# One weight load of a decode kernel, issued as two DMAs of 100 and 28 partitions

## The chip, the core and the metric

The kernel runs on one core of a Trainium2 chip. The metric is the device time of one execution in microseconds (us). The core has TensorE (PE in the profile), VectorE (DVE), ScalarE (ACT), GpSimd (POOL) and SyncE (SP), each with its own list of instructions; they meet at semaphores. Here SP issues nearly all DMAs, and sixteen DMA engines carry the bytes between HBM and the on-chip memory of 128 partitions.

## The reference

One decode step of a transformer block, for four sequences of one token each, width 512, in bfloat16:

```
x    = A_x                                                  # (4, 1, 512)
q    = layernorm(x) @ wq                                    # 32 heads of 128
p    = softmax(q . k_cache * 128**-0.5)                     # caches (4, 32, 8192, 128)
h    = x + (p . v_cache) @ wo
hn   = layernorm(h)
out  = h + (sigmoid(hn @ w_gate) * (hn @ w_up)) @ w_down    # 512 -> 1792 -> 512
```

The two caches are 512 MiB together; all weights are some 13 MB.

## The kernel before

**Attention.** The 128 pairs of sequence and head are taken four at a time, so there are 32 units (`NU`). A unit's K and its V are 8 MiB each and come in one DMA each into one of three slots of the tensor `KV`. For each unit DVE transposes K in chunks (L320), PE forms the scores (L329), DVE and ACT form the softmax (L336 to L356), and PE multiplies with V of the unit before (L368, L381). The loads are written in one fixed order in SP's list (`order`, L224): K of unit 0, then K of the next unit and V of the one before in turn. Each waits until its slot is free. The last V comes in two halves (L492).

**The tail.** When the last K has been read (`k_done`, L335 of the last unit), SP issues the weights into that slot: `wo` in two DMAs (L501), `w_gate` in one (L503) and `w_up` in two (L507). Then, when the slot of V is free (`v_done`), `w_down` follows in four (L512). All go through one queue, in this order, without a wait between them but `v_done`. `w_up` lies as 128 partitions of 4 x 1792 elements; the cut `WUC = (0, 3, 4)` gives the first load three of the four chunks `c` (10752 B a partition) and the second load one (3584 B a partition). `w_down` is cut at `WDT = (0, 4, 8, 12, 14)` of its fourteen tiles `t`.

The tail's arithmetic: PE finishes attention and multiplies with `wo` (L431), DVE and ACT form the layernorm (L266 to L270), PE transposes the result (L276), then multiplies with `w_gate` and `w_up` (both L446, four chunks `c` each). ACT takes the sigmoid (L457), which needs a table load first. DVE multiplies (L463) and transposes (L466), in two halves of seven tiles. PE multiplies with `w_down` (L471, two matmuls for each of fourteen tiles), the tiles in order, each group waiting for its load. DVE adds `h` (L477), and two small DMAs write the output (L514).

**Semaphores.** `prog.token(key, 16)` (L27) raises the count that a key is expected to reach by 16 and gives the value to wait for; `prog.dma` (L82) issues a DMA that adds 16 to the semaphore of that key when it is complete. The token of the second up load is `t_wu[1]`; PE's second group of up matmuls (L460) waits for it.

## Time and profile before

| | |
|---|---|
| median of 3 runs | 1281.62 us (1281.55 to 1281.74) |
| the profiled execution's own time | 1281.89 us |
| its span, first to last instruction | 1280.1 us |
| DMA | 550.83 MB, mean 430 GB/s |
| PE busy, matmuls | 789.8 us (62%) |
| DVE busy | 797.5 us (62%) |
| ACT busy | 55.2 us (4%) |
| mean granted TensorE clock | 0.811 of full speed |
| second up load: size, median issue to landing | 448 KB, 21.1 us |

The times in profile and trace are counted in us from the first instruction of the span. The page gives busy time by engine, then the span in 40 equal slices with a digit each (9 is 90% or more busy), then the DMA queues with packets, MB and their share of the time of sixteen DMA engines. The chain of work that ended last is followed back from the last instruction, at each step to what released it. In a timeline a row is start, length, engine, line, operation, tile and count, and in brackets how long the engine sat idle before it and what ended that. SPq is SP issuing DMAs: the length of such a row is the issue, not the transfer. Beside these views the trace holds every packet of the DMA engines (start, length, bytes, queue, but no engine number), and every increment of a semaphore by a DMA, here called a landing event.

### The profile page before, as it was taken

The page shows a single profiled execution, that of the slowest core. Times are in us where ns is not written, and L with a number is a line of the kernel's source. Part 1 is how long each engine was busy: PE and PEld are TensorE (multiplying, and loading weights), DVE is VectorE, ACT ScalarE, POOL GpSimd, SP SyncE. Part 2 cuts the span into 40 slices and gives each one's busy share as a digit, 9 for nine tenths or more (in the row PEclk, how much of TensorE's full clock was granted, in tenths as well). Part 3 has the DMA queues.
Part 4 walks back from the last instruction along what each step waited for, and adds up shares of the span by engine and source line. Part 5 has one row for each costly group of instructions (what it writes and reads, how often), then busy time and mean ns, then how long its engine had stood idle before and what let it go on. Part 6 is the DMA issues. An engine that isn't in the chain of part 4 may idle for free. (4 is left out here: it accounts for less than half of the span.)

```text
span 1280.1 us, 10700 instructions
## 1 busy us (share of the span) xinstructions
PE 789.8 (62%) x4485; PEld 292.0 (23%) x4485; DVE 797.5 (62%) x1075; ACT 55.2 (4%) x112; POOL 4.3 (0%) x18
## 2 busy tenths in 40 slices
PE   1676755557755557655557655567655577555586
PEld 0122212222212222212222212222122222122232
DVE  1876675567675567665567665566765666755671
ACT  2000000000000000000000000000000000000001
POOL 1000000000000000000000000000000000000000
PEclk8888877788877788877788877788777888777887
DMA  9999999999999999999999999999999999999998
GB/s 420 431 425 428 451 430 428 426 442 440 426 428 432 451 426 428 428 451 430 428 426 440 442 426 428 432 451 426 428 428 448 432 428 426 440 442 426 428 426 341
DMA packets 11596, 550.83 MB, mean 430 GB/s; under 512 B 1212, under 2 KB 1224, under 8 KB 2888
## 3 DMA queue, kind: packets, MB, share of 16 engines
q1 hardware_dynamic: 11576, 550.77, 99.6%
q8 instruction: 3, 0.05, 0.0%
q10 hardware_dynamic: 16, 0.01, 0.0%
q14 instruction: 1, 0.01, 0.0%
HBM read 550.77 MB, written 0.00 MB: 430 GB/s over the span
## 5 line engine op out<-in xcount | busy, mean ns | idle before, releaser
L329 PE MATMUL PS<-kT,Lq 128*128 128x512 bf16 x2048 | 587.9, 419 | 439.0 <-DVE kT L320 420.6
L320 DVE STREAM_TRANSPOSE kT<-KV 128x1024 f32<-128x1024 f32 x512 | 612.1, 1230 | 239.5 <-DMA KV<-in_A_k_cache_dram 192.1
L329 PEld LDWEIGHTS PS<-kT,Lq 128*128 128x128 bf16 x2048 | 176.9, 104 | 848.3 <-DVE kT L320 684.4
L368 PE MATMUL PS<-KV,PTz 128*16 128x512 bf16 x2048 | 120.5, 389 | 6.7 <-DVE PTz L349 3.5
L386 DVE STREAM_TRANSPOSE kT<-PS 128x128 f32<-128x128 f32 x32 | 10.1, 317 | 161.3 <-PE PS L381 161.3
L349 DVE STREAM_TRANSPOSE PTz<-E_sb 32x512 bf16<-32x512 bf16 x128 | 89.7, 701 | 3.6 <-ACT E_sb L343 0.6
L381 PE MATMUL PS<-kT,selw 128*128 128x128 f32 x256 | 66.3, 415 | 24.9 <-ACT kT L377 24.9
L368 PEld LDWEIGHTS PS<-KV,PTz 128*16 128x16 bf16 x2048 | 59.4, 110 | 65.6 <-issue 16.4
L343 ACT ACTIVATE E_sb<-PS,negm 128x512 bf16<-128x512 f32 x32 | 22.0, 687 | 1144.5 <-DVE negm L341 1144.5
L381 PEld LDWEIGHTS PS<-kT,selw 128*128 128x128 f32 x256 | 49.8, 206 | 43.9 <-ACT kT L377 40.8
L336 DVE TENSOR_REDUCE part<-PS 128x1 f32<-128x512 f32 x32 | 22.1, 692 | 35.8 <-PE PS L329 35.8
L377 ACT ACTIVATE kT<-PS 128x512 f32<-128x512 f32 x32 | 19.1, 598 | 61.1 <-PE PS L368 61.1
L387 DVE TENSOR_SCALAR OT<-kT,rsb 128x4 f32 (+1 forms) x32 | 7.3, 229 | 4.4
L313 DVE TENSOR_TENSOR Lq<-q_all,mask 128x32 bf16<-128x32 bf16 x32 | 9.6, 301 | 0.0
L431 PE MATMUL PS<-KV,OT 128*4 128x512 bf16 x32 | 8.4, 429 | 0.0
L341 DVE STREAM_TRANSPOSE negm<-mxr 128x32 f32<-128x32 f32 x32 | 6.8, 213 | 1.1
L338 DVE STREAM_TRANSPOSE turn<-part 128x32 f32<-128x32 f32 x32 | 6.8, 211 | 1.1
L356 DVE STREAM_TRANSPOSE rsb<-sgr 128x32 f32<-128x32 f32 x32 | 6.8, 211 | 1.1
L353 DVE STREAM_TRANSPOSE turn<-part 128x32 f32<-128x32 f32 x32 | 6.8, 212 | 1.0
L294 PE MATMUL PS<-KV,kT 128*4 128x512 bf16 x32 | 3.6, 627 | 5.4 <-DMA KV<-in_A_wq_dram 5.4
L339 DVE TENSOR_SCALAR_CACHE_REDUCE turn<-turn 128x32 f32<-128x32 f32 x32 | 5.9, 186 | 1.1
L301 DVE STREAM_TRANSPOSE kT<-PS 128x512 f32<-128x512 f32 x2 | 1.4, 717 | 8.2 <-PE PS L294 8.2
(52 smaller groups left out, 54.6 us busy)
## 6 DMA issues: line engine op xcount, KB each, us to landing
KV<-in_A_v_cache_dram SPq DMA_DIRECT2D x2, 4096.0 KB, 45.3
KV<-in_A_wq_dram SPq DMA_DIRECT2D x1, 4096.0 KB, 12.5
KV<-in_A_wo_dram SPq DMA_DIRECT2D x2, 2048.0 KB, 25.2
KV<-in_B_w_gate_dram SPq DMA_DIRECT2D x1, 1792.0 KB, 31.3
KV<-in_B_w_down_dram SPq DMA_DIRECT2D x3, 512.0 KB, 21.2
KV<-in_B_w_up_dram SPq DMA_DIRECT2D x1, 1344.0 KB, 23.2
KV<-in_A_k_cache_dram SPq DMA_DIRECT2D x32, 50.1
KV<-in_A_v_cache_dram SPq DMA_DIRECT2D x31, 31.4
```

What stands on the lines that cost most here:

```text
L313: t_lq[u] = emit("dve", lambda e, i: e.tensor_tensor(dst, bass.AP(raw(q_all), i * (4 * TU) + 4 * (u - TU * t), [[NU * 4, 128], [1, 4], [0, ...
L320: t_tr[u, c] = emit("dve", lambda e: e.transpose(kT[:, (c % 2) * TW:(c % 2 + 1) * TW], KVw[:, o:o + TW]), w, ch="d2p")
L329: ins = e.matmul(bank[SBK], Lq[:, 128 * t + 15 - c:128 * t + 143 - c], rhs, start=(c == 0 and t == 0), stop=(c == NT - 1 and t == 3))
L336: a = emit("dve", lambda e: e.tensor_reduce(part[:, 0:1], bank[SBK], AX.X, ALU.max), [t_sc[u, NT - 1], t_pool], ch="d2d")
L343: t_exp[u] = emit("act", lambda e: e.activation(E_sb[:, :], bank[SBK], ACT.Exp, bias=negm[:, 0:1], scale=SCALE, accum_out=part[:, 1:2]), [ ...
L349: return [e.transpose(PTz[32 * q:32 * (q + 1), :].rearrange("p (r q c) -> p r q c", r=4, q=4)[:, :, q, :], E_sb[32 * q:32 * (q + 1), :].re ...
L368: made.append(e.matmul(PS[32 * j:32 * j + 16, ob:ob + 512], lhsT, KV[:, slot * SLOT + 512 * k:slot * SLOT + 512 * (k + 1)], start=(k < 4), ...
L377: t_ocp[u] = emit("act", lambda e: e.activation(O_sb, bank[OBK], ACT.Copy), [t_pv[u]], ch="a2p")
L381: return e.matmul(bank[EX][:, 0:128], selw[:, q:q + 128], rhs, start=(q == 0), stop=(q == 3))
L386: a = emit("dve", lambda e: e.transpose(OTf[:, :], bank[EX][:, 0:128]), [t_ex[u]], ch="d2d")
L387: t_ot[u] = emit("dve", lambda e, i: e.tensor_scalar(bass.AP(raw(OT), i * (4 * TU) + 4 * (u - TU * t), [[NU * 4, 128], [1, 4]]), OTf[:, 0: ...
L431: ins = e.matmul(h_ps, OT[:, B * g:B * (g + 1), j], wo_v[:, g, j, :], start=False, stop=(g == 7 and j == 3), skip_group_check=True)
```

## The change

The second load of `w_up`, 128 partitions of 3584 B, is issued as two DMAs, one of partitions 0 to 99 and one of partitions 100 to 127, one right after the other. Both add 16 to the same semaphore. Its token is raised by another 16, so PE waits for 32. The first load of `w_up`, and all others, stay as they were. Lists of the other engines are the same as before, in order and in waits, apart from the value that PE waits for.

```diff
         t_wu = [prog.token(f"wu{i}", 16) for i in range(len(WUC) - 1)]
         t_vh = [prog.token(f"vh{i}", 16) for i in range(2)]
+        t_wu[-1] = prog.token(f"wu{len(WUC) - 2}", 16)
...
         for i in range(len(WUC) - 1):
-            prog.dma("sp", f"wu{i}", lambda e, i=i: e.dma_start(
-                reg(1, 16384 + (NC + WUC[i]) * F, (WUC[i + 1] - WUC[i]) * F), wu_src[:, WUC[i] * F:WUC[i + 1] * F]),
-                     [k_done], tok=t_wu[i])
+            for a, b in ((0, 100), (100, 128)) if i == len(WUC) - 2 else ((0, 128),):
+                prog.dma("sp", f"wu{i}", lambda e, i=i, a=a, b=b: e.dma_start(
+                    reg(1, 16384 + (NC + WUC[i]) * F, (WUC[i + 1] - WUC[i]) * F)[a:b], wu_src[a:b, WUC[i] * F:WUC[i + 1] * F]),
+                         [k_done], tok=t_wu[i])
```

## The prediction

> **What bounds the kernel now.** I read the whole span first, then the chain of work that ended last, then the last microseconds, and last the landing events of single DMAs. The page, slices and queues:

> ```profile
> span 1280.1 us, 10700 instructions
> DMA  9999999999999999999999999999999999999998
> q1 hardware_dynamic: 11576, 550.77, 99.6%
> ```

> All 40 slices of the span have the sixteen DMA engines at 90% or more, and one queue, SP's, fills 99.6% of their time. So no engine's arithmetic decides, but the stream of bytes, and an edit pays only by what it moves at the stream's end. The chain of work, in order of time, ends so:

> ```profile
> 1236.72 11.32 SPq L503 DMA_DIRECT2D KV<-in_B_w_gate_dram  x1
> 1248.09 4.37 SPq L507 DMA_DIRECT2D KV<-in_B_w_up_dram  x2
> 1252.50 6.14 SPq L512 DMA_DIRECT2D KV<-in_B_w_down_dram  x4
> ```
> ```profile
> 1254.21 21.99 DMA KV<-in_B_w_down_dram
> 1276.20 0.04 issue
> 1276.24 1.33 PE PS L471 x12
> 1277.57 0.02 issue
> 1277.60 0.42 DVE KV L477
> ```

> The first fence is SP's timeline: columns are start, length, work. L503 held SP for 11.32 us although L501's two issues took 0.93: SP waits for room in the queue. Its last issue ends at 1258.64, the data of w_down land 18 us later. The second fence is the chain: the end hangs on a part of w_down landing at 1276.20, then matmuls, then DVE's sum. PE's timeline agrees that it waited for that DMA:

> ```profile
> 1274.30 1.29 PE L471 MATMUL PS<-KV 128*4 128x256 bf16 x16 [1.28 <-DVE KV L466]
> 1276.24 1.29 PE L471 MATMUL PS<-KV 128*4 128x256 bf16 x12 [0.65 <-DMA KV<-in_B_w_down_dram]
> ```

> Which engines are late there? The DMA view of 1273 to 1277 us, in slices of 0.1 us:

> ```profile
> DMA  9999989998885913102302113021111000000000
> ```

> Up to 1274.3 nearly all sixteen are busy; from 1274.4 to 1276.4 one to three tenths of them, that is two to four engines, still work. The landing events say it exactly. Each load of 128 partitions raises its semaphore sixteen times, once per DMA engine. For the second up load the sixteen come, after the first at 1269.97, at

> ```
> 0 .04 .09 .15 .20 .31 .32 .33 .35 .38 .43 .48 .48 | 1.45 2.14 2.43 us
> ```

> The last parts of w_down have the same pattern: thirteen engines within 0.5 us, three stragglers 1.45, 2.14 and 2.43 behind the first. They are not slower: the pattern was the same to 0.05 us at 1176, 100 us earlier. They were set back once: at the first load (12.5 us) the three were at .56, .57 and .81, and code fetches in the DMA records at 53.83 (16 KB), 65.87 (8 KB) and 87.88 us (16 KB) are followed by steps of 1.55, 0.97 and 1.5. As the queue never runs empty, the delay stays to the end, where the last two parts of w_down land at 1276.20 and 1276.82 while the thirteen others had the first of these by 1274.30. A fourth fetch at 1274.33 held one more engine to about 1276.5.

> **The change, part by part.** One SP instruction of 128 rows becomes two, of 100 and 28; nothing else differs on any engine's list. Bytes, rows (3584 B each) and addresses are equal; PE's wait asks for 32 in place of 16.

> *SP.* One issue more. Issues on a free queue took 0.38 to 0.51 us here, the second up load 1.17, a blocked one 3.15. So 0.4 to 3.2 us later for the four w_down issues behind it, and for nothing else (SP's next is the output at 1278). Cover: 18 us between the last issue and its landing. Cost nothing; without that cover all of it.

> *PE's wait.* The last c of the up matmuls began at 1272.47, the load was in at 1272.40. The next need is the sigmoid, whose table load (1.28 us from 1271.54) lets DVE's product start at 1273.41 anyway; a landing up to some 0.5 us later is hidden there.

> *Which engine moves which rows.* This is the point of price. The trace shows DMAs of 128 partitions with sixteen landings of equal shares (wq: eight packets on each of the sixteen engines), and DMAs of four partitions (x, the output) with four data packets and four landings beside one early event. So engines get equal shares and their number follows the partitions. With equal shares and at most sixteen engines, 100 rows go to ten engines, ten each, and 28 to fourteen, two each. I infer that; no DMA of 100 or 28 is in the trace. If a smaller DMA uses the same engines counted from one end, ten engines get 12 rows where they had 8, four get 2, two get none. The price of a row: the medians of the landings of the two up loads, 1270.31 - 1269.17 = 1.14 us for eight rows, 0.14 each. So ten engines end 4 x 0.14 = 0.57 us later, four end 6 x 0.14 = 0.86 us earlier, two end 1.14 us earlier, and all that follows on an engine moves with it.

> *What that makes of the end.* If the three stragglers are among the six relieved, the last w_down part comes at 1276.82 - 0.86 to 1.14 = 1275.68 to 1275.96; the ten loaded engines come at 1274.92 + 0.57 = 1275.49, still ahead of it. The fourth fetch then finds its engine done or nearly so, if that is a relieved one. After the last landing DVE's sum began 0.77 us later (1277.60 - 1276.82), so it would begin at 1276.45 to 1276.73. What is late next: DVE's transpose of the second half ends at 1274.97; fourteen matmuls follow in seven pairs, spaced 0.11 us at full clock and 0.21 at the clock of the last ones, and 0.42 for the last, so 1276.1 to 1276.8. That is so close behind that a straggler removed altogether would give little more. I take a gain of 0.95, between 0.86 and 1.1. The profiled execution took 1281.89 (1.8 around its span), so 1280.9; the median of the runs is 0.27 below it, 1281.62, so **1280.7**.

> Are the stragglers among the six? For it: the landings of the first load trail off in steady steps (0 to .43, then .56, .57, .81), as if engines were served in turn, and all code fetches hit those at the end of that row; a smaller DMA leaves out the end of a row first. The packet of x that took 384 ns ends at 2.16 us, and a wq packet starts at 2.157 on what must be the same engine, one of the four that x uses; it ends second or third of sixteen, so that one is no straggler. Against it: the stragglers' first packets started 3rd, 6th and 14th, so the row is not plain. By chance alone three of sixteen would all be in the six once in 28.

> **The rivals.**

> *1. The relief does not arrive; same time, 1281.6 (1281.2 to 1281.8).* Either 100 and 28 rows are spread over all sixteen engines, six to nine rows each, at most one row or 0.14 us more, or what limits is not the engine that sends but the place that receives: the rows still go to the same 128 partitions, and if each group of partitions is filled at a fixed rate, a group behind by 2.4 us stays behind, whoever sends. For it: a packet of 32768 B takes 1.21 us on all engines alike, a rate the trace cannot put down to one side. Against it: x's four packets, of neighbouring partitions, overlap, three of 1024 B in 99 ns (31 KB per us) beside 27 KB per us for one stream. [...]

> *2. Slower: a straggler is among the ten; 1281.9 to 1282.2.* The price is the same four rows. It decides as soon as one of the two latest engines carries 12 rows: 2.14 + 0.57 - 2.43 = 0.28 us later, or 0.57 for the latest. If senders also meet at the same partitions while the ten carry 100 rows, their ten rows (1.42 us) could take up to twice as long: 1282.2 + 1.4 = 1283.6 at worst. If only the third straggler is loaded, 1.45 + 0.57 = 2.02, still a gain of 0.4: 1281.2. For it: ten of sixteen engines are loaded, and the order of first packets above. [...] The trace has no engine numbers.

> *3. The two DMAs cost in themselves, some tenths of a us to 3.2: 1281.8 to 1284.8.* This needs the 18 us of cover to vanish, by SP stalling on ten queues that fill early. L503's 11.32 us shows such stalls, but they end with room, not with an idle DMA.

> **How the numbers follow.** Forecast, 1280.4 to 1281.0: 0.57. Rival 1: 0.15; the third straggler alone loaded (1281.2): 0.05; rival 2: 0.20; rival 3: 0.03. The predicted time is the likeliest, 1280.7. The range, 1280.2 to 1282.5, takes in all but the ends of rivals 2 and 3. A measurement of this kernel can tell about 0.2%, 2.6 us, from no change. Every case but the far end of rival 3 is inside that: faster 0.02, same 0.95, slower 0.03.

> **What would show it.** In the changed profile: eleven landing events (ten and one early) for the DMA of 100 rows, fifteen for that of 28; SP one issue more, and its last issue still more than 15 us before the last landing; the thirteen early engines of the w_down parts split into a group 0.57 later and some earlier; the last landing 0.9 to 1.1 us earlier after the up load's rows than before; PE's wait before L471's last matmuls shorter. Wrong, if the last landing keeps its 2.4 us behind the first (rival 1), grows to 2.7 or more (rival 2), or if stretches without DMA work appear before 1274 (rival 3).

## The result, and the profile after

| | before | changed |
|---|---|---|
| median of 22 runs | 1281.55 us (1280.93 to 1282.13) | 1283.58 us (1282.89 to 1284.39) |
| the profiled execution | 1281.89 us | 1282.97 us |

The ratio is 1.0016 with an interval of 1.001 to 1.0022: the kernel became 2.0 us slower. Forecast was 1280.7, so the sign was wrong as well. The profiled execution of the changed kernel is one of its fastest, only 1.08 us above the profiled one of before. At 1263 us, before the edit can act, its latest engine is also 0.57 us earlier than in the profile of before (a load is complete at 1263.16 in place of 1263.73). So what the tail lost in this execution is 1.08 us and up to 0.57 more, some 1.7 us at most.

The chain of work of the changed kernel ends, in order of time (start, length, what):

```profile
1251.31 2.40 SPq L509
1253.71 0.06 issue
1253.76 0.36 SPq L514
1254.12 0.05 issue
1254.17 0.65 SPq L514
1254.82 0.04 issue
1254.86 22.53 DMA KV<-in_B_w_down_dram
1277.39 0.04 issue
1277.43 1.44 PE PS L472 x8
1278.88 0.02 issue
1278.90 0.42 DVE KV L478
```

The chain still ends with w_down: its third part, then the last matmuls, then the sum. (The view counts eight matmuls there; twelve were left.) How little of that was a wait is told below. The lines of code are one or two higher than before. The two issues took 0.56 and 2.40 us, and w_down's last issue ended at 1257.38, 20 us ahead of its landing. So SP is not what cost. PE's timeline (start, length; in brackets its idle time and what ended that) shows the loss where the up load is used:

```profile
1270.46 0.93 PE L447 MATMUL PS<-KV,kT 128*4 128x448 bf16 x16 [0.27 <-DVE kT L281]
1272.06 1.29 PE L447 MATMUL PS<-KV,kT 128*4 128x448 bf16 x12 [0.67 <-DMA KV<-in_B_w_up_dram]
1273.88 0.54 PE L447 MATMUL PS<-KV,kT 128*4 128x448 bf16 x4 [0.52 <-DMA KV<-in_B_w_up_dram]
1275.52 3.31 PE L472 MATMUL PS<-KV 128*4 128x256 bf16 x28 [1.10 <-DVE KV L467]
```

PE now waits for both up loads; before, it passed all 32 matmuls of that line (L446 there) without a wait for DMA:

```profile
1271.33 1.69 PE L446 MATMUL PS<-KV,kT 128*4 128x448 bf16 x32 [0.27 <-DVE kT L280]
```

The last row of the changed kernel has all 28 matmuls of w_down in one run, where before they came in two, with 0.65 us of waiting for a load between them. PE's granted clock was lower there as well, 0.50 in place of 1.00, as the windows of one of these us show, first before, then changed:

```profile
1275.00:1276.00 1.00, 0.59 (x8) 0.26 (x8) 0.00 (x0) 0.00 (x0) 0.00 (x0) 1.00 0.17 57
1275.00:1276.00 1.00, 0.48 (x6) 0.32 (x8) 0.93 (x4) 0.00 (x0) 0.00 (x0) 0.50 0.83 324
```

The cause of the late up load is in the windows too. Columns are the stretch, busy time of the engines, then at the end the granted clock, the DMA engines' busy share and GB/s. Before:

```profile
1266.00:1268.00 2.00, 2.00 (x11) 0.77 (x9) 0.00 (x0) 0.00 (x0) 0.00 (x0) 1.00 0.99 418
1269.00:1273.00 4.00, 1.96 (x36) 0.88 (x36) 1.46 (x5) 2.49 (x5) 0.00 (x0) 1.00 1.03 410
```

The changed kernel:

```profile
1266.00:1268.00 2.00, 1.57 (x8) 0.42 (x5) 0.39 (x1) 0.00 (x0) 0.00 (x0) 1.00 0.98 412
1269.00:1273.00 4.00, 2.16 (x32) 0.74 (x32) 0.98 (x3) 2.57 (x4) 0.00 (x0) 0.85 1.01 239
```

The share of busy time is nearly the same, 1.03 and 1.01, but the bytes fell from 410 to 239 GB/s. The DMA engines did not run dry in the mean; packets took longer. The packets say how much longer: the 128 rows of 3584 B took 142 ns in the mean before and 234 now, with single ones up to 380. Their neighbours in time suffered too: the rows of the first up load rose from 408 to 428 ns, those of 4096 B from 163 to 174. Summed over the rows of all loads after 1230 us that is 29 us of engine time, or 1.8 us on each of sixteen engines in the mean; more than half of it fell on rows of other loads.

The landing events of the second up load are 26, which is what ten engines, fourteen engines and two early events give. That fits the two DMAs being dealt out as inferred. The DMA view of 1273 to 1279 us, in slices of 0.15 us:

```profile
DMA  9799999999989987978877663100000000000000
```

The long thin tail of before (one to three tenths for 2 us) is short now, and the last landing of w_down is at 1278.02, against 1276.82. Of the second of its four parts, four engines landed within 0.22 us, eleven 1.1 to 1.8 us after the first, the last 2.5.

### The profile page after: what moved, and what is told of

The parts are those of the page before. It is cut to its first block, busy times and chain, and to the rows that moved or that the text cites. A ratio compares the mean times of both kernels' runs of the same rounds, so it can differ in the third digit from the quotient of the medians.

```text
span 1281.3 us, 10701 instructions
## 1 busy us (share of the span) xinstructions
PE 790.9 (62%) x4485; PEld 292.3 (23%) x4485; DVE 797.1 (62%) x1075; ACT 55.2 (4%) x112; POOL 4.3 (0%) x18
## 2 busy tenths in 40 slices
DMA  9999999999999999999999999999999999999998
## 3 DMA queue, kind: packets, MB, share of 16 engines
q1 hardware_dynamic: 11584, 550.77, 99.7%
HBM read 550.77 MB, written 0.00 MB: 430 GB/s over the span
## 5 line engine op out<-in xcount | busy, mean ns | idle before, releaser
L344 ACT ACTIVATION_READ_ACCUMULATOR E_sb<-PS,negm 128x1 f32 x32 | 6.2, 193 | 0.0
## 6 DMA issues: line engine op xcount, KB each, us to landing
KV<-in_A_wq_dram SPq DMA_DIRECT2D x1, 4096.0 KB, 12.2
```

Of the source, the lines that this page charges most:

```text
L344: t_exp[u] = emit("act", lambda e: e.activation(E_sb[:, :], bank[SBK], ACT.Exp, bias=negm[:, 0:1], scale=SCALE, accum_out=part[:, 1:2]), [ ...
```

## The experiments

Three theories, to be told apart by times and rows, since no trace has engine numbers. **M, meeting:** in a load of 128 partitions each engine writes partitions of its own; in any other cut by partitions several engines at a time write into one group of partitions, which is supposed to have one way in (a path of fixed rate), and share that rate. **T, tilt:** ten engines carry four rows more and come later. **D:** a second DMA on the same semaphore costs by itself.

The small kernels cut the same up load in other places. For the cut at 96 (and 64, 112) one number of the change differs:

```diff
+            for a, b in ((0, 96), (96, 128)) if i == len(WUC) - 2 else ((0, 128),):
```

and the cut by columns is

```diff
+            for a, b in ((0, F // 2), (F // 2, F)) if i == len(WUC) - 2 else ((0, (WUC[i + 1] - WUC[i]) * F),):
...
+                    reg(1, 16384 + (NC + WUC[i]) * F, (WUC[i + 1] - WUC[i]) * F)[:, a:b],
+                    wu_src[:, WUC[i] * F + a:WUC[i] * F + b]), [k_done], tok=t_wu[i])
```

**By columns.** 

> The second up load in two DMAs on one semaphore, but cut by columns: each has all 128 partitions and 1792 B of each. Theory M (engines meet at the same partitions: rows of 3584 B rose from 142 to 234 ns with the cut at 100): every engine keeps the partitions it had, so nothing changes, 0 to +0.3 us. Theory T (tilt: ten engines carry four rows more): shares are equal, 0. Theory D (a second DMA on the same semaphore costs by itself, by its issue or the doubled wait): the +2.0 us of the changed kernel come back, 1283.6.

Measured 1281.24 us, ratio 0.9998 (0.9989 to 1.0007). Two DMAs on one semaphore cost nothing that can be measured (the interval ends at +0.9 us, D asks for +2.0): D falls. The rate stays:

```profile
1269.00:1273.00 4.00, 1.98 (x36) 0.88 (x36) 1.22 (x4) 2.77 (x5) 0.00 (x0) 1.00 1.04 405
```

**Cut at 96.** 

> The changed kernel with the cut at 96 in place of 100. 96 rows are six on each of sixteen engines, 32 are two on each, so every engine carries eight rows as before. Theory T: no tilt, so 0 against the kernel before. Theory M: the engines leave the partitions that they have in a load of 128 and meet others, so rows again take well over 142 ns and the time rises by 1 to 2 us. Theory D: +2.0.

Measured 1283.45 us, ratio 1.0015 (1.0005 to 1.0024), +1.9. By equal shares all engines carry eight rows (32 landing events fit that), and the price is that of the change. T is not needed for it. The rate (of this kernel) is down in the same way, and the rows of 3584 B took 224 ns:

```profile
1269.00:1273.00 4.00, 2.49 (x28) 0.83 (x32) 0.63 (x2) 2.57 (x4) 0.00 (x0) 0.63 1.00 249
```

**Cut at 64.** 

> Cut at 64: four rows on each of sixteen engines, twice. Theory T: 0. Theory M, if two engines share the way into each group of partitions at half speed: eight rows of 0.14 us take twice as long, +1.1 us, and what follows is disturbed as well. Theory D: +2.0.

Measured 1283.70 us, ratio 1.0017 (1.0008 to 1.0026), +2.2, twice the +1.1 expected for the rows alone. Rows took 267 ns, nearly twice 142, which is 1.0 us on each engine; the rows of the loads around them lengthened by another 1.9 us on each.

```profile
1269.00:1273.00 4.00, 2.16 (x24) 0.69 (x28) 0.38 (x2) 2.57 (x4) 0.00 (x0) 0.60 1.02 210
```

**Cut at 112.** 

> Cut at 112: seven rows and one row on each of sixteen engines. Theory T: 0. Theory M: slower again, by 1 to 2 us. Theory D: +2.0.

Measured 1282.70 us, ratio 1.001 (1.0001 to 1.0019), +1.2; rows took 225 ns. With a few tenths of scatter from run to run, these four tell that every cut by partitions costs and the cut by columns doesn't, but not one cut's price from another's. So the next kernels leave the up load whole and cut the second half of the last V, nine times the bytes (the cut by columns has a loop over two column ranges instead):

```diff
-                    prog.dma("sp", f"vh{i}", lambda e, src=src, slot=slot, i=i: e.dma_start(
-                        reg(slot, i * SLOT // 2, SLOT // 2), src[:, i * SLOT // 2:(i + 1) * SLOT // 2]), [w], tok=t_vh[i])
+                    for d, s in zip(parts, parts) if i else ((slice(0, 128), slice(0, 128)),):
+                        prog.dma("sp", f"vh{i}", lambda e, src=src, slot=slot, i=i, d=d, s=s: e.dma_start(
+                            reg(slot, i * SLOT // 2, SLOT // 2)[d], src[s, i * SLOT // 2:(i + 1) * SLOT // 2]), [w], tok=t_vh[i])
```

Here `parts` stands for the list of slices, which the kernels write out, and the token is raised by 16 for each DMA more. The kernel before moves, in the stretch of this load, the following:

```profile
1246.00:1250.00 4.00, 3.30 (x32) 1.07 (x32) 1.40 (x5) 0.00 (x0) 0.00 (x0) 0.50 1.07 459
```

**V by columns.** 

> The same half of the last V cut by columns, two DMAs of 128 partitions and 16384 B each. All theories but D: 0. Theory D: +2.

Measured 1281.49 us, ratio 0.9999 (0.999 to 1.0009). D falls here too.

```profile
1246.00:1250.00 4.00, 3.61 (x32) 1.08 (x32) 0.84 (x5) 0.00 (x0) 0.00 (x0) 0.50 1.00 426
```

**V cut at 64.** 

> The kernel before, but the second half of the last V (128 partitions of 32768 B, 4 MiB, 9.7 us of the stream) comes in two DMAs of 64 partitions on one semaphore; the up load is whole. Theory M with a way that passes 27 B per ns for each group: rows take 2.42 us in place of 1.21 and the time rises by some 9.7 us. Theory T: four rows on every engine twice, 0. Theory D: 0 to +2.

Measured 1293.63 us, ratio 1.0093 (1.0076 to 1.011), +12.1. The rate is half, and the 128 rows of this load took 2.52 us in the mean, against 1.22:

```profile
1246.00:1250.00 4.00, 3.48 (x32) 0.92 (x28) 0.60 (x4) 0.00 (x0) 0.00 (x0) 0.52 1.12 229
```

That fits M with two engines on each way. The 2.4 us above the expected 9.7 are mostly rows a little longer than double (0.8 us on each engine) and rows of 4096 B that met the last rows of V (163 to 180 ns in the mean, 1.4 us on each engine).

**V cut at 100.** 

> The same half of the last V cut at 100 and 128. Theory T alone: ten engines carry four rows of 1.21 us more, +4.8 us at most, less what the relieved engines take off the stragglers. Theory M: that and the meeting; scaled by bytes from the +2.0 us of 448 KB, 4096 KB give some +18 us. Theory D: +2.0, since the count of DMAs is that of the changed kernel.

Measured 1308.27 us, ratio 1.0206 (1.0188 to 1.0224), +26.7, where T allows 4.8. M's +18, scaled by bytes, was low. The rate shows that of these three cuts of V the one of the change is the worst:

```profile
1246.00:1250.00 4.00, 0.75 (x8) 0.36 (x12) 1.30 (x5) 0.00 (x0) 0.00 (x0) 0.50 0.83 95
```

Rows took 3.29 us in the mean, fifteen of them 4.9 to 5.1, four times 1.22.

The last three put tilt and meeting apart, and the side that is read from the side that is written. Each has sixteen DMAs of eight partitions, so that by the inferred equal shares eight engines carry sixteen rows. For steps, `parts` is `[slice(32 * g + j, 32 * g + j + 29, 4) for g in range(4) for j in range(4)]`, for neighbours `[slice(8 * g, 8 * g + 8) for g in range(16)]`; the third reads by the second list and writes by the first.

**Eight partitions, four apart.** 

> The second half of the last V in sixteen DMAs of eight partitions, each four apart (0, 4 ... 28, then 1, 5 ... 29 and so on). Eight engines carry one row of 1.21 us of each, so sixteen rows in place of eight. Theory T (shares alone): +9.7 us. Theory M: the eight rows of a DMA go to eight different groups of four partitions and hardly meet each other; +9.7 to +20 us, since the other eight engines, with later loads, are met in the upper half of the partitions.

Measured 1294.14 us, ratio 1.01 (1.0083 to 1.0116), +12.5.

```profile
1246.00:1250.00 4.00, 3.61 (x32) 1.06 (x32) 1.08 (x5) 0.00 (x0) 0.00 (x0) 0.50 1.05 434
```

The rate holds at first, and 87 of the 128 rows of this load kept their 1.22 us, nearly all of its first half among them. This is the tilt nearly by itself: 8 rows x 1.21 = 9.7. The rest is longer rows in the second half of the load, which goes to the upper partitions (mean row of all 1.43 us); that these met later loads, as M says, is not shown.

**Eight neighbours.** 

> The same sixteen DMAs of eight partitions, but of neighbours (0 to 7, 8 to 15 and so on). Shares are as in the one before, so theory T: the same time, +9.7 us. Theory M, if four neighbours share one way: four rows at a time through each of two ways, rows of 4.8 us, +60 to +70 us.

Measured 1323.59 us, ratio 1.0305 (1.0261 to 1.0349), +42.0. The four runs spread from 1315.08 to 1328.90 us, and the slowest is the profiled one. The same rows and counts, and 29 us more: only the choice of partitions differs.

```profile
1246.00:1250.00 4.00, 2.41 (x24) 1.07 (x28) 0.67 (x4) 0.00 (x0) 0.00 (x0) 0.50 0.97 135
```

The expected +60 was too much: rows took 3.5 us, not 4.8. That would fit three engines on a way, as if one of four drifted ahead to the next group; no run shows how many there were.

**Neighbours read, steps written.** 

> Reads the rows of the neighbours (as the one with neighbours) and writes them to partitions four apart (as the one with steps); the rows of this half of V so come to wrong partitions. If the meeting is at the partitions written, the time is that of the steps; if it is in the rows read, that of the neighbours.

Measured 1294.81 us, ratio 1.0104 (1.0087 to 1.0121), +13.2: the time of the steps. So what costs is the choice of the partitions written, not of the memory read.

```profile
1246.00:1250.00 4.00, 3.13 (x32) 0.83 (x24) 0.32 (x2) 0.00 (x0) 0.00 (x0) 0.61 0.97 401
```

The sum can now be made for all cuts by partitions: the lengthening of the rows of all loads after 1230 us, divided by sixteen engines, and the tilt (rows more on the loaded engines).

| kernel | mean row of the cut load, uncut | lengthening / 16 | tilt | sum | measured, medians | measured, that execution |
|---|---|---|---|---|---|---|
| the change | 234 ns, 142 | 1.8 us | 0.57 | 2.4 | +2.0 | +1.1 |
| up load at 96 | 224, 142 | 1.9 | 0 | 1.9 | +1.9 | +1.6 |
| up load at 64 | 267, 142 | 2.9 | 0 | 2.9 | +2.2 | +2.8 |
| up load at 112 | 225, 142 | 1.9 | 0 | 1.9 | +1.2 | +1.5 |
| V at 64 | 2516, 1217 | 11.9 | 0 | 11.9 | +12.1 | +13.0 |
| V at 100 | 3289, 1217 | 24.2 | 4.8 | 29.0 | +26.7 | +28.1 |
| V, eight by steps | 1433, 1217 | 3.8 | 9.7 | 13.5 | +12.5 | +12.2 |
| V, eight neighbours | 3505, 1217 | 33.4 | 9.7 | 43.1 | +42.0 | +47.0 |
| V, eight mixed | 1440, 1217 | 4.0 | 9.7 | 13.7 | +13.2 | +12.5 |

The lengthening comes from one profiled execution each. The last column has the time of that same execution, less the 1281.89 us of the profiled one of before. The sums agree with it within 1.3 us, except for eight neighbours, where 3.9 us stay unexplained. So the sum tells the large cuts apart well, and gives only the size of the small ones.

## Why the prediction was wrong

*The bound* was right: the stream of bytes, and its end in w_down. So was *SP*: an issue more cost nothing under 20 us of cover, and the two cuts by columns show that the second DMA and the doubled count cost nothing measurable.

*How the rows are dealt out* was right as far as the trace tells: 26 landing events, as ten, fourteen and two. With V cut at 100, w_gate, which comes later, lands in two groups, six engines within 2.4 us and ten 11.9 to 13.1 us after the first, as six relieved and ten loaded engines would.

*The step that failed* is "The price of a row": 0.14 us, taken from a load of 128 partitions and carried over to loads of 100 and 28. A row took 0.23 us there, and made the rows of other loads longer as well. In place of 0.57 us more on ten engines and 0.86 to 1.14 less on six, rows lengthened by 1.8 us on each engine in the mean (how this was shared between loaded and relieved ones the trace does not tell). The cut at 96 has no tilt and no relief and gives the same time, so neither decides it. That the price hangs on which partitions are written at a time is shown by the kernels with eight (+42.0 us for neighbours, +13.2 where the same rows were written four apart); for the cut at 100 it is taken over from there, with the same sign, longer rows.

*The stragglers* may in part have been where I put them; it did not help. In the kernel with eight partitions by steps, the load before the cut one has its latest engines 0.78, 0.93, 1.76 and 1.83 us behind the first. Of the first DMA of eight, the eight landings end 0.78 and 0.94 behind: the two latest engines are not among those eight. In the changed kernel the thin tail shortened, which fits with two of them among the six relieved; in that execution, though, the latest engine lagged less before the edit as well, by 1.80 us and not 2.43. That they were relieved, and what the relief was worth, is argued and not shown.

*PE's wait* was costed at nothing, with a cover of some 0.5 us, and this term failed with the first. The load came at 1273.83 in place of 1272.40, so the cover was used up, and DVE's product began at 1274.63 in place of 1273.41. The matmuls of w_down then began at 1275.52 in place of 1274.30 and ran nearly without a stop: their pairs start 0.21 us apart at the clock of 0.50 (before, 0.11 while the clock was 1.00), and only the pair that needed the third part came 0.47 after the one ahead of it. By that spacing the lateness of w_down cost some 0.2 us at the end, an estimate; its fourth part, in at 1278.02, was not waited for, since PE came to it at 1278.24. The chain names w_down, but by this the late up load alone would have brought the end nearly as far. Both loads are late by the same lengthened rows.

*Rival 1* had a fixed rate into each group of partitions, which the runs fit, but drew "same time" from it. The bytes of each group are indeed the same; but if several engines stand at one way, other ways carry nothing meanwhile. The 239 GB/s of the window, with all engines busy, agree with that, and so do the 2.52 us of rows cut at 64 and the 29 us between steps and neighbours. The groups and their ways no trace shows. I had set against it x's three packets (31 KB per us beside 27): 3 KB in 99 ns is too short to show a rate.

*Rival 2* had the right sign, and in a clause the right price: if senders meet, rows "could take up to twice as long", 1283.6 at worst. I took that for an extreme and ended the range at 1282.5. It was no extreme, since with a cut at 100 rows take 2.7 times as long where there are enough of them (V). That 1283.6 meets the measured 1283.58 is luck: the up load's rows took 1.65 times as long, not twice, and the rest came from rows of other loads. The chance that this rival gave to the stragglers belonged to the meeting.

## What to carry to other kernels

Where the DMA engines are the bound, as here with one queue at 99.6% of their time, cut a load along the bytes of each partition, not across partitions: into two DMAs, the first cost nothing measurable at 448 KB and at 4 MiB, the second 1.2 to 2.2 us at 448 KB and 12 to 27 us at 4 MiB. A busy share near 1 says nothing of bytes moved (1.03 went with 410 GB/s, 1.01 with 239), so read GB/s beside it, and the length of packets of one size. And a price taken from one shape of transfer is not the price of another shape until a trace has it (0.14 us a row in a load of 128 partitions, 0.23 when it was cut at 100).

## What the runs showed that I had not expected

In the profile of before, code fetches of 16 KB are followed by a delay of some 1.5 us of what I take for one DMA engine each, and nothing made it good in the next 1200 us: the latest landing of a load was 2.33 us behind the first at 109 us and 2.43 at 1270, and from 90 to 1274 us SP's queue filled 100.0% of the engines' time. In the changed kernel's profile the same fetches leave the latest engine 1.8 us behind the first in place of 2.4. That makes the 0.57 us by which its loads were complete earlier, with no part of the edit in it.
